# Weights taken apart and put together in alternate steps, block stores ahead of the v and r loads, and unread products between the steps of the first four chains

## Chip, cores and metric

One core of one Trainium2 chip. The metric is the device time of one execution in microseconds (us). "Clock" is TensorE's granted clock as the profile records it, as a share of full speed: 0.50 is half, 1.00 is full.

## The reference, cut to what matters

```python
def _attn_ref(r, k, v, w, a, b):                  # B, H, S, D = 4, 8, 768, 40
    state = zeros((B, H, D, D))
    for t in range(S):
        y[:, :, t] = einsum('bhd,bhde->bhe', rt, state)
        Sa = einsum('bhde,bhe->bhd', state, at)
        state_decay = state * wt[:, :, None, :] - einsum('bhd,bhe->bhde', Sa, bt)
        state = state_decay + einsum('bhd,bhe->bhde', vt, kt)
    return y

def _moe_ref(x, w_in, w_out):                     # x: 3072 x 320, w_in: 320 x 2048, w_out: 2048 x 320
    h = x @ w_in
    return (h / (1 + exp(-h))) @ w_out

out = _moe_ref(y.transpose(0, 2, 1, 3).reshape(B * S, H * D), ...)
```

All of it is in float32.

## The kernel before

The recurrence is cut into 12 chunks of 64 tokens. The parts that matter here are these.

- **Inversion.** For every pair of chunks VectorE (DVE) inverts small triangular blocks row by row (31 rows, two instructions each). Inversion 1 serves chunks 0 and 1, inversion 3 chunks 2 and 3, inversion 5 chunks 4 and 5. Its result goes out to memory and comes back, and TensorE (PE) **merges** it (`pq`, then `po`).
- **Chain.** Each chunk then runs a chain of PE steps: transposes (`pt`), scores (`pm`, `pr`), solve (`pu`, `pw`), update (`pg`), read (`pl`), write (`py`), turn (`pt`). Most of these products are small, 64 rows or 64 columns.
- **MoE.** After every two chunks follow 16 steps with large products: 8 "first" (`ph`) and 8 "second" (`po`).
- **Weights.** 40 pieces arrive as bit patterns of 64-bit floats and are turned into float32 on DVE and ScalarE (ACT).

The order in which steps are written is a proposal: the scheduler that builds the program may place an instruction earlier on its engine if its inputs allow it. That is how MoE products get into PE's waits.

```python
def weave(*lists):                      # mixes lists of steps by their relative position
    at = [(i + 0.5) / len(x) for x in lists for i in range(len(x))]
    steps = [s for x in lists for s in x]
    for i in sorted(range(len(steps)), key=lambda i: at[i]):
        steps[i]()
# ... cut ...
for u in units[0]:
    load_rv(u)                          # loads of r and v
run(prepare(0))
# ... cut ...
run(prepare(1))                         # stores the blocks (md) for inversion 1
# ... cut ...
run(steps[0:1] + convert[0:8] + steps[1:32])            # inversion 1 with 8 weight pieces
# ... cut ...
    weave(late.pop(0) + steps, convert[8:20])           # merge 1 (second half), chain 0
# ... cut ...
    weave(steps[0:4], convert[20:24])                   # chain 1
    weave(steps[4:], convert[24:34], prepare(2))
fetch, queue = moe(0, xs)
# ... cut ...
    weave(queue[0:12], prepare(3) + convert[34:] + invert(3))
del queue[0:12]
for n in range(2, NN):
    # ... cut ...
    steps = [x for pair in zip(*[chain(u, xs) for u in units[n]]) for x in pair]
    steps[4:4] = late.pop(n, [])
    now = 8 if n > 3 else 0
    weave(steps[0:4], queue[0 : now // 4])
    weave(steps[4:], queue[now // 4 : now], prepare(n + 2) + invert(n + 2))
    del queue[0:now]
```

`invert(n)` ends with the merge, so the merge of inversion 5 is written at the end of chain 3.

Of the kernel before, what the change touches and what calls it, by code (L numbers as in the profile page):

```python
# [9 lines left out]
F32 = mybir.dt.float32  # L10
I32 = mybir.dt.int32
U32 = mybir.dt.uint32
# [29 lines left out]
def kernel(  # L42
# [79 lines left out]
    for half in range(2):  # L122
# [6 lines left out]
        for c in range(NF * DM // 2 * half, NF * DM // 2 * (half + 1), WS):  # L129
            pieces.append((wo_f[:, c : c + WS], [(0, 128, w_out[:, 2 * c : 2 * (c + WS)])]))  # L130
    NW = len(pieces)
    rooms = {}

    def load_weights(n):

        if n == 0:
            rooms["gts"] = sb.tile([128, 4, 4 * WS], I32, name="room4", tag="gts")
        if n < NW // 2 and n % 5 < 4:
            rooms[n] = rooms["gts"][:, n % 5]
        else:  # L140
            tag = "room" if n < NW // 2 else ("room", "mi", "tmp")[n % 3]
            rooms[n] = sb.tile([128, 4 * WS], I32, name="room", tag=tag)
        for lo, hi, src in pieces[n][1]:
            raw = rooms[n][lo:hi, 0 : 2 * WS]
            nc.sync.dma_start(raw.rearrange("p (i x) -> p i x", x=256) if len(src.shape) == 3 else raw, src)

    def weights(n):
        dst, room = pieces[n][0], rooms[n]
        words = room[:, 0 : 2 * WS].rearrange("p (c two) -> p c two", two=2)
        lo, hi = words[:, :, 0], words[:, :, 1]  # L150
        e, f = room[:, 2 * WS : 3 * WS], room[:, 3 * WS : 4 * WS]
        shr, band, bor = ALU.logical_shift_right, ALU.bitwise_and, ALU.bitwise_or
        nc.vector.tensor_scalar(out=e, in0=hi, scalar1=20, scalar2=0x7FF, op0=shr, op1=band)
        nc.vector.tensor_scalar(out=f, in0=hi, scalar1=0xFFFFF, scalar2=None, op0=band)
        nc.scalar.activation(out=e, in_=e, func=AF.Relu, scale=2.0**23, bias=low)
        nc.scalar.activation(out=f.bitcast(F32), in_=f, func=AF.Copy, scale=2.0**-20, bias=1.0)  # L156
        nc.scalar.activation(out=lo.bitcast(F32), in_=lo.bitcast(U32), func=AF.Copy, scale=2.0**-52)
        nc.vector.scalar_tensor_tensor(out=e, in0=hi, scalar=-(1 << 31), in1=e, op0=band, op1=bor)
        f, lo, e = (x.bitcast(F32) for x in (f, lo, e))
        nc.vector.tensor_tensor(out=f, in0=f, in1=lo, op=ALU.add)  # L160
        nc.vector.tensor_tensor(out=dst, in0=f, in1=e, op=ALU.mult)
        ahead = 5 if n + 5 < NW // 2 else 3
        if n + ahead < NW and (n + 5 < NW // 2 or n + ahead >= NW // 2):
            load_weights(n + ahead)
# [109 lines left out]

    def inverse(md):
        steps = []
# [21 lines left out]
        def back():  # L298
            nc.sync.dma_start(zd, XI)
            turned = XI.rearrange("p t s -> p s t")  # L300
            nc.scalar.copy(out=mi[:, 0:16], in_=turned[:, 0:16])
            nc.vector.tensor_copy(out=mi[:, 16:32], in_=turned[:, 16:32])
            nc.sync.dma_start(xd, mi)

        steps.append(back)
        return steps, xd, zd

    def merge(n, xd, zd):
        X = XT[n % 2].rearrange("p m h t -> p (m h) t")
# [3 lines left out]
        def fetch():  # L313
            for be in range(2):
                at = 64 * (n % 2) + 32 * be
                nc.sync.dma_start(X[C * be : C * be + 32, :, 32:64], zd[at : at + 16].rearrange("q t s -> t q s"))
                for c in range(2):
                    r = C * be + 32 * c
                    nc.sync.dma_start(
                        X[r : r + 32, :, 32 * c : 32 * c + 32],  # L320
# [319 lines left out]
    def invert(n):  # L640

        if n >= NN or n % 2 == 0:
            return []
        box = {}

        def begin():
            box["rows"], box["xd"], box["zd"] = inverse(md[0])

        def do(k, i):
            if i == 0:  # L650
                box[k] = merge(k, box["xd"], box["zd"])
            box[k][i]()
# [8 lines left out]
    def run(steps):  # L661
        for step in steps:
            step()
# [4 lines left out]
    for n in range(5):  # L668
        load_weights(n)
    convert = [partial(weights, n) for n in range(NW)]  # L670
    xs = dr.tile([DM, 4 * NM * C], F32, name="xs", bufs=2)
    for u in units[0]:
        load_rv(u)
    run(prepare(0))
    for t in RHS + Gbd + GT + XT:
        nc.gpsimd.memset(t, 0.0)
    run(prepare(1))
    chains = {0: [chain(u, xs) for u in units[0]]}
    run([x[i] for i in range(2) for x in chains[0]])
    steps = invert(1)  # L680
    run(steps[0:1] + convert[0:8] + steps[1:32])
    queue = []
    with tc.issue_after(mark["row"]):
# [3 lines left out]
        steps = [x for pair in zip(*[x[2:] for x in chains[0]]) for x in pair]  # L687
        weave(late.pop(0) + steps, convert[8:20])
        for u in units[1]:
# [3 lines left out]
        steps = [x for pair in zip(*[chain(u, xs) for u in units[1]]) for x in pair]  # L693
        weave(steps[0:4], convert[20:24])
        weave(steps[4:], convert[24:34], prepare(2))
    fetch, queue = moe(0, xs)
    fetch()
    with tc.issue_after(mark["turn"]):
        weave(queue[0:12], prepare(3) + convert[34:] + invert(3))
    del queue[0:12]  # L700
    for n in range(2, NN):
# [8 lines left out]
        now = 8 if n > 3 else 0  # L710
        weave(steps[0:4], queue[0 : now // 4])
        weave(steps[4:], queue[now // 4 : now], prepare(n + 2) + invert(n + 2))
        del queue[0:now]
# [160 lines left out]
```

## Time and profile before

| | us |
|---|---|
| median of 3 runs | 977.7 (977.1 to 979.0) |
| the profiled run | 991.1, of the slow state |

The page of the kernel before gives busy time per engine, and then groups of instructions: line, engine, operation, tile written and tiles read, shapes, count, busy us and mean ns, and the engine's idle time just before them.

```profile
PE 849.9 (86%) x10914; PEld 597.4 (60%) x10914; DVE 581.3 (59%) x1045; ACT 281.1 (28%) x628; POOL 92.9 (9%) x90
...
L589 PE MATMUL ph<-xt,wi_s 128*128 128x512 f32 x384 | 197.2, 645 | 30.8 <-DVE gts L598 18.7
L605 PE MATMUL po<-wo_s,gts 128*128 128x320 f32 x768 | 214.5, 436 | 0.0
```

PE is the busiest engine, and over half of its busy time is MoE products (the two groups below and 58.0 us of another first-step group, L594). Note the count of 768: 6 MoE blocks with 8 second steps of 8 products each are 384 products in the source, so **each float32 product leaves two records** in the trace.

### The profile page before, as it was taken

The numbers are of one execution on the slowest core, as the hardware profiler recorded it, in microseconds if no ns is written. First come the engines' busy times: TensorE is split into PE (matmuls) and PEld (weight loads), VectorE is DVE, ScalarE is ACT, GpSimd is POOL, SyncE is SP. The second block draws the span as 40 slices with busy tenths as digits, with TensorE's granted clock in tenths as the row PEclk, the third lists the DMA queues.
The fourth block names the chain that finished last, engine by engine and source line by source line (L and its number), as shares of the span: only waits on it lengthen the run. The fifth ranks groups of instructions, "written<-read, shape, count | busy, mean of one in ns | idle before, by whom it ended". The sixth has DMA issues, their size and how long they took to land. (4 is left out here: it accounts for less than half of the span.)

```text
span 989.2 us, 25109 instructions
## 1 busy us (share of the span) xinstructions
PE 849.9 (86%) x10914; PEld 597.4 (60%) x10914; DVE 581.3 (59%) x1045; ACT 281.1 (28%) x628; POOL 92.9 (9%) x90
## 2 busy tenths in 40 slices
PE   0302989687999778999989999989999999999996
PEld 0302989434489663677745786637867558755544
DVE  8699386998713579526797165991467934031111
ACT  2513453441131412243212433112342033310110
POOL 6101001120000201001120001010020000000000
PEclk9855575899995789999999999999999999999999
DMA  9755255520133560335441345503534133002001
GB/s 227 174 150 138 68 145 133 156 66 17 46 80 95 135 151 13 75 92 126 113 102 56 74 116 125 136 24 76 129 90 115 37 75 82 6 14 58 1 0 30
DMA packets 208948, 87.68 MB, mean 89 GB/s; under 512 B 169408, under 2 KB 199616, under 8 KB 208832
## 3 DMA queue, kind: packets, MB, share of 16 engines
q1 hardware_dynamic: 204608, 84.97, 34.9%
q8 instruction: 87, 1.43, 0.6%
q10 hardware_dynamic: 4224, 1.05, 0.6%
q14 instruction: 29, 0.24, 0.1%
HBM read 68.68 MB, written 17.30 MB: 87 GB/s over the span
## 5 line engine op out<-in xcount | busy, mean ns | idle before, releaser
L589 PE MATMUL ph<-xt,wi_s 128*128 128x512 f32 x384 | 197.2, 645 | 30.8 <-DVE gts L598 18.7
L605 PE MATMUL po<-wo_s,gts 128*128 128x320 f32 x768 | 214.5, 436 | 0.0
L605 PEld LDWEIGHTS po<-wo_s,gts 128*128 128x128 f32 x768 | 143.5, 190 | 64.1 <-issue 3.8
L589 PEld LDWEIGHTS ph<-xt,wi_s 128*128 128x128 f32 x384 | 70.2, 198 | 124.1 <-issue 65.7
L598 DVE TENSOR_TENSOR gts<-ph,sg 128x512 f32<-128x512 f32 x96 | 63.6, 681 | 112.1 <-ACT sg L597 111.9
L597 ACT ACTIVATE sg<-ph 128x512 f32<-128x512 f32 x96 | 52.7, 594 | 226.6 <-PE ph L594 226.6
L286 DVE TENSOR_TENSOR tmp<-XI,mi 128x1 f32<-128x1 f32 (+30 forms) x186 | 100.0, 537 | 11.0 <-DMA mi<-md 6.0
L292 DVE TENSOR_REDUCE XI<-tmp 128x1 f32<-128x1 f32 (+30 forms) x186 | 93.3, 501 | 5.0
L216 PE MATMUL pm<-a,kb 64*64 64x64 f32 x1536 | 45.7, 240 | 39.5 <-POOL kb L248 20.6
L248 POOL TENSOR_TENSOR kb<-kb,w 128x512 f32<-128x512 f32 x42 | 50.4, 1222 | 252.5 <-DVE w L245 185.4
L245 DVE RECIPROCAL w<-W 128x512 f32<-128x512 f32 x21 | 70.3, 3346 | 0.6
L331 PE MATMUL pq<-XT,sb 32*32 32x32 f32 x768 | 26.1, 199 | 50.0 <-DMA XT<-zd 50.0
L216 PEld LDWEIGHTS pm<-a,kb 64*64 64x64 f32 x1536 | 36.8, 148 | 50.8 <-POOL kb L248 41.0
L224 DVE TENSOR_TENSOR sk<-pm,ms 128x256 f32<-128x256 f32 x48 | 18.2, 419 | 82.3 <-PE pm L216 82.3
L246 POOL TENSOR_TENSOR a<-a,W 128x512 f32<-128x512 f32 x24 | 29.1, 1212 | 394.9 <-DMA a<-in_aT 212.4
L515 PE MATMUL pl<-r,vut 64*128 64x64 f32 x768 | 60.6, 310 | 0.0
L507 ACT COPY GT<-pt 40x512 f32<-40x512 f32 x44 | 25.5, 579 | 122.7 <-PE pt L498 121.9
L515 PEld LDWEIGHTS pl<-r,vut 64*128 64x128 f32 x768 | 58.8, 223 | 1.6 <-issue 0.9
L594 PE MATMUL ph<-xt,wl_s 64*128 64x512 f32 x192 | 58.0, 671 | 0.5 <-DMA xt<-xs 0.5
L331 PEld LDWEIGHTS pq<-XT,sb 32*32 32x32 f32 x768 | 23.6, 115 | 56.4 <-ACT room L156 49.9
L485 DVE TENSOR_TENSOR Gbd<-pg,Gbd 64x320 f32<-64x320 f32 x44 | 21.5, 488 | 57.4 <-PE pg L476 56.4
L553 DVE TENSOR_TENSOR yx<-py,W 64x512 f32<-64x512 f32 x48 | 33.0, 688 | 26.2 <-PE py L542 25.4
(97 smaller groups left out, 1026.8 us busy)
## 6 DMA issues: line engine op xcount, KB each, us to landing
a<-in_aT SPq DMA_DIRECT2D x24, 256.0 KB
kb<-in_bT SPq DMA_DIRECT2D x48, 128.0 KB
kb<-in_kT SPq DMA_DIRECT2D x48, 128.0 KB
vut<-in_vT SPq DMA_DIRECT2D x48, 128.0 KB
r<-in_rT SPq DMA_DIRECT2D x24, 256.0 KB
w<-in_wT SPq DMA_DIRECT2D x40, 128.0 KB
room<-in_w_out SPq DMA_DIRECT2D x20, 256.0 KB
room<-in_w_in SPq DMA_DIRECT2D x16, 256.0 KB
```

Source lines behind the costliest of these rows:

```text
L216: nc.tensor.matmul(pm[j][C * be : C * be + C, p * C : p * C + C], lhsT=u.kb[J, q, n, :], rhs=u.a[J, q, :], start=True, stop=True,)
L245: nc.vector.reciprocal(R, u.W[:, :, 1 : C + 1])
L248: nc.gpsimd.tensor_tensor(out=u.kb[:, :, n], in0=u.kb[:, :, n], in1=R, op=ALU.mult)
L286: nc.vector.tensor_tensor(out=tmp[:, 0:n, 0:n], in0=XI[:, t + 1 : 32, t + 1 : 32], in1=mi[:, t, t + 1 : 32].unsqueeze(1).to_broadcast([128 ...
L292: last = nc.vector.tensor_reduce(out=XI[:, t + 1 : 32, t], in_=tmp[:, 0:n, 0:n], axis=AX.X, op=ALU.add)
L331: nc.tensor.matmul(pq[be][r + 32 : r + 64, h * 32 : h * 32 + 32], lhsT=s[r : r + 32, h, 32:64], rhs=X[r : r + 32, h, 32:64], start=True, s ...
L515: nc.tensor.matmul(pl[j][:, q * C : q * C + C], lhsT=u.vut[J, q].rearrange("p n t -> p (n t)"), rhs=u.r[J, q, :], start=True, stop=True,)
L589: in_order(nc.tensor.matmul(ph[n], lhsT=wi_s[:, k, at : at + 128], rhs=xt[:, k, :], start=k == 0, stop=False))
L594: in_order(nc.tensor.matmul(ph[n], lhsT=wl_s[R, i, :], rhs=xt[R, 2, :], start=False, stop=True))
L597: nc.scalar.activation(out=sg, in_=ph[n], func=AF.Sigmoid)
L598: nc.vector.tensor_tensor(out=box["gts"][:, (2 * i + n) % (NF // 2), :], in0=ph[n], in1=sg, op=ALU.mult)
L605: in_order(nc.tensor.matmul(po[:, 0:DM], lhsT=box["gts"][:, f, b * 128 : b * 128 + 128], rhs=wo_s[:, NF // 2 * half + f, :], start=f == 0, ...
```

## The change

The intent is to start the first inversion earlier, to keep VectorE free of conversions while it inverts, and to keep the TensorE clock up in chains 0 to 3 with large products that nobody reads. Five parts:

1. One step takes piece n apart and puts piece n-1 together, so that DVE does not wait for ACT inside a piece; 24 pieces instead of 20 use the early rooms; the first five loads go out on ACT's queue.
2. r and v of the first chunk are loaded after the block stores.
3. Inversion 1's copies use ACT's queue, and merge 1's second half comes four steps into the chain.
4. Conversions are dealt out anew: 6 in inversion 1 (8 before), 13 in chain 0 (12), 7 in chain 1 (14), 15 in the first MoE block (6).
5. **Fillers**: 38 unread products of 512 columns, kept in program order: 10 before merge 1 and one after every second step of chains 0 to 3 (28).

```diff
     def weights(n):
-        # whole piece n: shift, mask, three ACT steps, or, add, multiply
+        if n < NW:
+            # take piece n apart: shift, mask, three ACT steps
+        n -= 1
+        # put piece n-1 together: or, add, multiply
# ... cut ...
-    def inverse(md):
+    def inverse(md, queue):
-            nc.sync.dma_start(xd, mi)
+            queue.dma_start(xd, mi)             # ACT's queue for inversion 1
# ... cut ...
-        load_weights(n)
-    convert = [partial(weights, n) for n in range(NW)]
+        load_weights(n, nc.scalar)
+    convert = [partial(weights, n) for n in range(NW + 1)]
+
+    def busy(x, times=1):
+        for _ in range(times):
+            pj = moe_bank("pj")
+            tc.keep_in_program_order(nc.tensor.matmul(pj, lhsT=ident, rhs=x, start=True, stop=True))
+
+    still = partial(busy, one.rearrange("p q t -> p (q t)")[:, 0:512])
+
+    def with_busy(steps):
+        return [y for i, x in enumerate(steps) for y in ([x, still] if i % 2 else [x])]
# ... cut: load_rv(units[0]) moves behind the start of inversion 1 ...
-    run(steps[0:1] + convert[0:8] + steps[1:32])
+    run(convert[0:6] + steps[1:32])
+    busy(XI.rearrange("p s t -> p (s t)")[:, 0:512], 10)
# ... cut ...
-        weave(late.pop(0) + steps, convert[8:20])
+        steps[4:4] = late.pop(0)
+        weave(with_busy(steps), convert[6:19])
# ... cut ...
-        weave(steps[0:4], convert[20:24])
-        weave(steps[4:], convert[24:34], prepare(2))
+        weave(with_busy(steps[0:4]), convert[19:21])
+        weave(with_busy(steps[4:]), convert[21:26], prepare(2))
# ... cut ...
-        weave(queue[0:12], prepare(3) + convert[34:] + invert(3))
+        weave(queue[0:12], prepare(3) + convert[26:] + invert(3))
# ... cut ...
+        if n < 4:
+            steps = with_busy(steps)
+        cut = 4 if n > 3 else 6
-        weave(steps[0:4], queue[0 : now // 4])
-        weave(steps[4:], queue[now // 4 : now], prepare(n + 2) + invert(n + 2))
+        weave(steps[0:cut], queue[0 : now // 4])
+        weave(steps[cut:], queue[now // 4 : now], prepare(n + 2) + invert(n + 2))
```

More of the change, by code (lines that the diff above doesn't have):

```diff
@@ L130, with load_weights @@
             pieces.append((wo_f[:, c : c + WS], [(0, 128, w_out[:, 2 * c : 2 * (c + WS)])]))
-    NW = len(pieces)
+    NW, NG = len(pieces), 24
     rooms = {}
-    def load_weights(n):
+    def load_weights(n, queue=nc.sync):
         if n == 0:
             rooms["gts"] = sb.tile([128, 4, 4 * WS], I32, name="room4", tag="gts")
-        if n < NW // 2 and n % 5 < 4:
+        if n < NG and n % 5 < 4:
             rooms[n] = rooms["gts"][:, n % 5]
         else:
-            tag = "room" if n < NW // 2 else ("room", "mi", "tmp")[n % 3]
+            tag = "room" if n < NG else ("room", "mi", "tmp")[n % 3]
             rooms[n] = sb.tile([128, 4 * WS], I32, name="room", tag=tag)
@@ L144, in load_weights, with parts @@
             raw = rooms[n][lo:hi, 0 : 2 * WS]
-            nc.sync.dma_start(raw.rearrange("p (i x) -> p i x", x=256) if len(src.shape) == 3 else raw, src)
-    def weights(n):
-        dst, room = pieces[n][0], rooms[n]
-        words = room[:, 0 : 2 * WS].rearrange("p (c two) -> p c two", two=2)
-        lo, hi = words[:, :, 0], words[:, :, 1]
-        e, f = room[:, 2 * WS : 3 * WS], room[:, 3 * WS : 4 * WS]
-        shr, band, bor = ALU.logical_shift_right, ALU.bitwise_and, ALU.bitwise_or
-        nc.vector.tensor_scalar(out=e, in0=hi, scalar1=20, scalar2=0x7FF, op0=shr, op1=band)
-        nc.vector.tensor_scalar(out=f, in0=hi, scalar1=0xFFFFF, scalar2=None, op0=band)
-        nc.scalar.activation(out=e, in_=e, func=AF.Relu, scale=2.0**23, bias=low)
-        nc.scalar.activation(out=f.bitcast(F32), in_=f, func=AF.Copy, scale=2.0**-20, bias=1.0)
-        nc.scalar.activation(out=lo.bitcast(F32), in_=lo.bitcast(U32), func=AF.Copy, scale=2.0**-52)
+            queue.dma_start(raw.rearrange("p (i x) -> p i x", x=256) if len(src.shape) == 3 else raw, src)
+    shr, band, bor = ALU.logical_shift_right, ALU.bitwise_and, ALU.bitwise_or
+    def parts(n):
+        words = rooms[n][:, 0 : 2 * WS].rearrange("p (c two) -> p c two", two=2)
+        return words[:, :, 0], words[:, :, 1], rooms[n][:, 2 * WS : 3 * WS], rooms[n][:, 3 * WS : 4 * WS]
+    def weights(n):
+        if n < NW:
+            lo, hi, e, f = parts(n)
+            nc.vector.tensor_scalar(out=e, in0=hi, scalar1=20, scalar2=0x7FF, op0=shr, op1=band)
+            nc.vector.tensor_scalar(out=f, in0=hi, scalar1=0xFFFFF, scalar2=None, op0=band)
+            nc.scalar.activation(out=e, in_=e, func=AF.Relu, scale=2.0**23, bias=low)
+            nc.scalar.activation(out=f.bitcast(F32), in_=f, func=AF.Copy, scale=2.0**-20, bias=1.0)
+            nc.scalar.activation(out=lo.bitcast(F32), in_=lo.bitcast(U32), func=AF.Copy, scale=2.0**-52)
+        n -= 1
+        if n < 0:
+            return
+        lo, hi, e, f = parts(n)
         nc.vector.scalar_tensor_tensor(out=e, in0=hi, scalar=-(1 << 31), in1=e, op0=band, op1=bor)
@@ L160, in weights @@
         nc.vector.tensor_tensor(out=f, in0=f, in1=lo, op=ALU.add)
-        nc.vector.tensor_tensor(out=dst, in0=f, in1=e, op=ALU.mult)
-        ahead = 5 if n + 5 < NW // 2 else 3
-        if n + ahead < NW and (n + 5 < NW // 2 or n + ahead >= NW // 2):
+        nc.vector.tensor_tensor(out=pieces[n][0], in0=f, in1=e, op=ALU.mult)
+        ahead = 5 if n + 5 < NG else 3
+        if n + ahead < NW and (n + 5 < NG or n + ahead >= NG):
             load_weights(n + ahead)
@@ L302, in back, with merge @@
             nc.vector.tensor_copy(out=mi[:, 16:32], in_=turned[:, 16:32])
-            nc.sync.dma_start(xd, mi)
+            queue.dma_start(xd, mi)
         steps.append(back)
         return steps, xd, zd
-    def merge(n, xd, zd):
+    def merge(n, xd, zd, queue):
         X = XT[n % 2].rearrange("p m h t -> p (m h) t")
@@ L318, in fetch @@
                     r = C * be + 32 * c
-                    nc.sync.dma_start(
+                    queue.dma_start(
                         X[r : r + 32, :, 32 * c : 32 * c + 32],
@@ L644, in invert @@
         box = {}
+        queue = nc.scalar if n == 1 else nc.sync
         def begin():
-            box["rows"], box["xd"], box["zd"] = inverse(md[0])
+            box["rows"], box["xd"], box["zd"] = inverse(md[0], queue)
         def do(k, i):
             if i == 0:
-                box[k] = merge(k, box["xd"], box["zd"])
+                box[k] = merge(k, box["xd"], box["zd"], queue)
             box[k][i]()
@@ L668 @@
     for n in range(5):
-        load_weights(n)
-    convert = [partial(weights, n) for n in range(NW)]
+        load_weights(n, nc.scalar)
[7 more added lines that the diff above has]
+        return [y for i, x in enumerate(steps) for y in ([x, still] if i % 2 else [x])]
     xs = dr.tile([DM, 4 * NM * C], F32, name="xs", bufs=2)
-    for u in units[0]:
-        load_rv(u)
     run(prepare(0))
@@ L677 @@
     run(prepare(1))
+    steps = invert(1)
+    run(steps[0:1])
+    for u in units[0]:
+        load_rv(u)
     chains = {0: [chain(u, xs) for u in units[0]]}
     run([x[i] for i in range(2) for x in chains[0]])
-    steps = invert(1)
-    run(steps[0:1] + convert[0:8] + steps[1:32])
+    run(convert[0:6] + steps[1:32])
+    busy(XI.rearrange("p s t -> p (s t)")[:, 0:512], 10)
     queue = []
```

## The prediction

> **What bounds the kernel now.** I read the forty-slice strip first, because it shows where the engines change roles; then a table of busy time by stage, cut where one kind of work ends on VectorE (DVE) or TensorE (PE); then PE's waits; then the timelines around the worst places. The strip, one digit per 24.7 us, in tenths:
>
> ```profile
> PE   0302989687999778999989999989999999999996
> ...
> DVE  8699386998713579526797165991467934031111
> ...
> PEclk9855575899995789999999999999999999999999
> ```
>
> PE is nearly empty for four slices while DVE is full. PE is then full at a granted clock of about a half, dips near slices 7 to 9, and from about slice 17 on is full at full clock. The stage table has for each stretch its length, the busy us (and instruction count) of PE, weight load, DVE, ACT and POOL, then clock, DMA share and GB/s:
>
> ```profile
> 45.80:83.00 37.20, 0.00 (x0) 0.00 (x0) 35.27 (x78) 5.45 (x14) 0.00 (x0) 0.50 0.49 127
> 83.00:105.60 22.60, 13.20 (x258) 12.96 (x258) 16.07 (x37) 11.77 (x25) 3.87 (x3) 0.50 0.56 152
> 105.60:180.00 74.40, 70.94 (x1072) 68.16 (x1072) 50.90 (x120) 34.24 (x87) 4.01 (x3) 0.61 0.48 128
> 180.00:283.90 103.90, 86.49 (x423) 44.88 (x418) 81.38 (x144) 31.03 (x69) 12.11 (x10) 0.92 0.27 66
> 283.90:360.30 76.40, 68.66 (x1507) 64.13 (x1504) 33.88 (x55) 22.08 (x51) 9.36 (x8) 0.75 0.44 106
> 360.30:424.00 63.70, 53.91 (x261) 27.67 (x261) 46.82 (x75) 14.18 (x29) 4.89 (x4) 0.92 0.31 73
> 424.00:989.20 565.20, 544.81 (x7136) 369.20 (x7134) 282.59 (x478) 146.25 (x314) 38.27 (x32) 0.99 0.30 73
> ```
>
> In order: the first triangular inversion (DVE alone), merging its result, chains 0 and 1, the first MoE block with inversion 3, chains 2 and 3, inversion 5, and the rest. PE bounds the chains, at a reduced clock; DVE bounds the inversions; after 424 us PE is busy 544.8 of 565.2 us, so **any PE work pushed behind that point adds its full length**. The wait view and two timelines carry the rest:
>
> ```profile
> PE pq L331 <- DMA XT<-zd: 50.0, 2, 49.8
> ```
> ```profile
> 92.90 3.35 DVE L245 RECIPROCAL w<-W 128x512 f32<-128x512 f32 x1
> 97.03 0.58 ACT L341 COPY qq<-pq 32x512 f32<-32x512 f32 x1
> 153.55 12.20 PE L515 MATMUL pl<-r,vut 64*128 64x64 f32 x64
> 442.78 3.79 PE L515 MATMUL pl<-r,vut 64*128 64x64 f32 x64
> ```
>
> PE waits 49.8 us for the first merge. Inside it ACT, in order, sits behind a 3.35 us reciprocal before it can evacuate the second merge product. The same 64 products take 12.20 us at half clock and 3.79 us at full clock. The profiled run took 991 us, the unprofiled median is 977.7; I work in the trace's time and carry differences over.
>
> **What the Trainium skill says.** "TensorE: Matmul & The Clock Gate", Part 1, has an idle PE at 1.2 GHz and a busy one at 2.4 GHz after about 3.4 us. The trace agrees on two levels (0.50 and 1.00) but not on what counts as busy: from 100 to 120 us PE is 100% busy with 64-row products at 0.50. [...]The same page, Part 2 (step 1), keeps matmuls in program order, only weight loads being pulled ahead; the 49.8 us wait agrees. "DMA: Bandwidth & Descriptors", "Issuing engines are not separate DMA queues", says that a second issuing engine saves only issue time: here that is 3.55 us for six weight loads and about 9 us for the r and v loads that stand before the 16 block stores (`md`). "Advanced Engine Details and Errata", "VectorE Performance Modes", says GpSimd and two-port VectorE instructions block each other: the conversion's first step has median 0.285 us and maximum 1.27 us.
>
> **The change, part by part.**
> (1) *Blocks ahead of r and v.* The last score is ready at 31.2 us; four stores at 0.57 us each and the weights' `w` reach 34.1; the read-back's second half goes after the last store has landed, about 36.1, and lands 3.8 us later as now. Inversion 1 starts at about 40 instead of 45.8: **-6**.
> (2) *Fewer conversions inside inversion 1.* Its 62 row instructions are 31.4 us busy plus about 2 us of gaps; with 1.3 us of other work it ends at about 75 instead of 83 (2 us gained).
> (3) *Merge.* The copies back go out on ACT's queue, and only the first merge precedes the first solve. Result read-back 6.5 us, ten filler products during it, one merge at full clock and the copies: 13.5 us instead of 22.6, so the solve starts near 88 instead of 105.6: **-17**.
> (4) *Chains 0 and 1.* At full clock a chain pair costs PE 28.4 us including its merge (after 424: 544.8 minus 34 first products at 4.82 and 36 second products at 4.36, over 8 pairs). From 88: 56 us of PE work with 13 fillers at 0.47, against 76 us of DVE work counted from 75 on. With some 10 us of stalls: end at about 156 instead of 180: **-24**.
> (5) *First MoE block.* 15 conversions, about 2 us each, fall here instead of 6 to 9. Summing the row durations in the order of the built program, DVE has 47.7 us before inversion 3 and 39.1 us inside it, plus 4 us of waits: inversion 3 ends at 247 instead of 267.4. Chain 2 starts 12 us later, 259 instead of 283.9: **-25**.
> (6) *Chains 2 and 3.* Now 76.4 us, of which about 33 us are at half clock (16 us to be won) and 7.7 us idle. With 15 fillers at 0.47 (+7) and 2 us more waiting: about 70; end 329 instead of 360.3: **-31**.
> (7) *What the fillers lock out.* They are kept in program order, so nothing written after them in the source can be placed before them. Comparing the two built programs' PE order: before, by chain 4's first transpose 14 first and 12 second steps of the MoE are done; after, 8 and 4.75. None stands between chain 3 and the merge that needs inversion 5. DVE then needs 42 us for inversion 5 and read-back and merge 14 more: chain 4 starts at 329 + 42 + 14 = 385 instead of 424: **-39**, with PE idle for some 45 us which the kernel before fills with MoE products.
> (8) *The bill.* 6 first steps at 4.82 (28.9) and 7.25 second steps at 4.36 (31.6): **+60** behind chain 4, where PE is full. Of 20 us idle there some 6 may be filled by them: -6.
> Sum: -39 + 60 - 6 = +15. Parts (4) and (6) may each be 4 to 8 us better than I assume, hence +8 as my middle.
>
> **Rivals.** *A: the early gain reaches the end.* For it: 58.6 us of PE time are lost to the half clock (busy time times missing clock, summed over 10 us stretches), and PE idles 88 us before 106. Against it: part (7); to be 2% faster chain 4 would have to start near 350, while DVE's row durations up to the end of inversion 5 already sum to 312 us and chain 4 needs 14 more, with no idle DVE at all. It would make about 940 to 955. *B: the fillers do not hold the clock.* One of 0.45 us in every 4 to 5 us. Against it: from 424 on the clock is 0.99 although single MoE pairs are 10 us apart. If it held, parts (4) and (6) shrink by 20 us and the time is about 1005. *C: DVE bounds more than I sum*, by waits for weight loads with only three rooms in the first MoE block, or by GpSimd conflicts: 5 to 10 us later, about 995. *D: the locked-out MoE work fits into later waits of PE.* The order after chain 4 spreads it into the chains, but only 13 us of PE idleness before the tail is there to be filled; it is in the sum.
>
> **Range and chances.** Middle 986, from +8. The sum of seven stages, each good to 3 to 8 us, gives about 15 us either way; B and C stretch the upper side, A's milder forms the lower: 964 to 1006. Faster by over 2% (under 958) needs an error in (7) or (8): 0.12. Slower by over 2% (over 997): 0.28. Same: 0.60.
>
> **What would show it.** Inversion 1 from 40 to 75; first solve near 88; clock close to 1.00 from there to chain 4, but for the gaps in which PE idles; end of chain 1 near 156; chain 2's transposes near 259; chain 3's end near 329; then a PE wait of about 45 us for the inversion, absent before; chain 4 near 385; and from there 620 us to the end instead of 565. If PE works on the MoE between chains 3 and 4, or if the rest takes under 600 us, (7) or (8) is wrong and the kernel is faster than I say. If the clock stays at a half in chains 0 to 3, B is right.

## More of the kernel before

A run counts as slow when it is over 1.5% above the fastest run of the same kernel.

## The result and the profile after

The changed kernel is correct and takes **1031.6 us** (median of 4 runs, 1030.9 to 1036.8) against 977.4 us in the same rounds. The ratio is 1.0574, with a 95% interval from 1.0524 to 1.0624: slower by 5.7%, and outside the predicted range. Ratios here are the mean time of one kernel's fast runs over that of the other's fast runs of the same rounds, in the experiments without the profiled runs, so they are not quite the ratio of the quoted medians.

The strip of the changed kernel, one digit per 25.7 us, in tenths:

```profile
PE   0418996892996506999998999999999999999997
...
DVE  8997686988053792163597164893446934122211
...
PEclk9757688996698856999999999899999999999999
```

PE has a hole in slices 14 and 15 (digits 5 and 0) that the kernel before has not, and the clock falls to 5 and 6 tenths in slices 15 and 16. (The 2 in slice 10 is a shorter wait, 20.7 us, for inversion 3.) From then on PE is full to the end. In slices 4 to 13 the clock is better than before in places, but not 1.00.

The views of PE's waits and of PE's instructions in order of time show the hole. The timeline columns are start, us, engine, line, tiles, shapes, count, and in brackets the idle time before and its releaser.

```profile
PE pq L339 <- DMA XT<-zd: 68.1, 2, 47.4
```
```profile
106.41 7.09 PE L523 MATMUL pl<-r,vut 64*128 64x64 f32 x64
...
394.74 3.40 PE L339 MATMUL pq<-XT,sb 32*32 32x32 f32 x64 [47.36 <-DMA XT<-zd]
398.07 2.08 PE L685 MATMUL pj<-one,ident 128*128 128x512 f32 x2
399.94 2.31 PE L613 MATMUL po<-wo_s,gts 128*128 128x320 f32 x5
```

PE stands idle for 47.4 us until inversion 5 is back, does that merge's first products, then **one filler**, and only then an MoE product (`po`). And at 106 us the 64 `pl` products take 7.09 us, at a clock of 0.50. So they do in chain 2 of the kernel before, in its first profile and also at 0.50:

```profile
305.84 7.09 PE L515 MATMUL pl<-r,vut 64*128 64x64 f32 x64
```

That is close to twice the 3.79 us at full clock. The 12.20 us which the prediction called half clock (chain 1, also recorded at 0.50) are more than half a clock explains; what made them so long is not known.

Because the first profile of the kernel before was of a slow run, I profiled it again (the first experiment). Its busy times by stage, with the columns of the prediction's stage table; the rows are the start up to the first solve, chains 0 and 1, from there to chain 2 (first MoE block, inversion 3), chains 2 and 3, from there to chain 4 (inversion 5), and chain 4 to the end:

```profile
0.00:105.12 105.12, 24.34 (x529) 22.78 (x529) 85.89 (x175) 33.21 (x79) 24.30 (x33) 0.70 0.68 162
105.12:172.95 67.83, 64.07 (x1074) 61.26 (x1072) 51.39 (x120) 34.37 (x88) 3.97 (x3) 0.71 0.52 141
172.95:276.05 103.10, 85.62 (x418) 45.08 (x417) 81.60 (x144) 30.98 (x69) 12.07 (x10) 0.90 0.26 66
276.05:348.53 72.48, 64.62 (x1507) 60.41 (x1504) 33.75 (x55) 22.03 (x51) 9.36 (x8) 0.81 0.46 112
348.53:412.25 63.72, 53.77 (x261) 27.65 (x261) 46.86 (x75) 14.22 (x29) 4.88 (x4) 0.92 0.32 73
412.25:977.20 564.95, 544.51 (x7137) 369.25 (x7134) 282.53 (x478) 146.30 (x314) 38.24 (x32) 0.99 0.30 73
```

The same six stages of the changed kernel:

```profile
0.00:89.25 89.25, 28.74 (x421) 20.65 (x421) 82.53 (x164) 26.19 (x64) 24.10 (x33) 0.76 0.78 179
89.25:163.86 74.61, 70.96 (x1225) 56.50 (x1225) 54.77 (x122) 38.72 (x98) 7.43 (x6) 0.76 0.50 133
163.86:265.15 101.29, 68.52 (x355) 34.68 (x355) 77.00 (x150) 33.18 (x75) 8.29 (x7) 0.83 0.29 74
265.15:347.39 82.24, 72.98 (x1534) 58.92 (x1532) 35.23 (x60) 22.24 (x51) 9.35 (x8) 0.88 0.42 101
347.39:406.50 59.11, 11.76 (x142) 8.75 (x142) 40.79 (x60) 7.14 (x15) 4.88 (x4) 0.57 0.27 65
406.50:1029.20 622.70, 602.83 (x7321) 402.46 (x7318) 287.71 (x492) 153.82 (x328) 39.07 (x32) 0.99 0.27 68
```

The first solve comes 16 us earlier. Chains 0 and 1, and chains 2 and 3, each take longer than before although their clock is higher. PE does 11.8 us of work in the 59.1 us ahead of chain 4, against 53.8 of 63.7. And what was not done there comes after chain 4: 622.7 us instead of 565.0, with PE busy for 602.8 instead of 544.5. These are 58 us more of PE work at the end; chain 4 starts 5.7 us earlier than before, so 52 us of loss are left between these two traces.

### The profile page after: what moved, and what is told of

It reads as the page before. It is cut to its first block, busy times and chain, and to the rows that moved or that the text cites. A ratio compares the mean times of both kernels' runs of the same rounds, so it can differ in the third digit from the quotient of the medians.

```text
span 1029.2 us, 25272 instructions
## 1 busy us (share of the span) xinstructions
PE 855.8 (83%) x10990; PEld 582.0 (57%) x10990; DVE 578.0 (56%) x1045; ACT 281.3 (27%) x628; POOL 93.1 (9%) x90
## 4 chain that ended last, share of the span: by engine, by line
PE 62%; DVE 28%; DMA 4%; issue 2%; ACT 2%; SPq 0%; POOL 0%; ACTq 0%; DVEq 0%; POOLq 0%
PE po L613 16%; PE ph L597 12%; DVE tmp L294 8%; DVE XI L300 7%; DVE w L253 4%; PE ph L602 4%; PE pj L685 3%; PE pl L523 3%; PE pu L446 3%; PE pm L224 2%; PE py L550 2%; PE pr L424 2%; PE py L543 2%; PE pq L339 2%; PE pg L484 2%
## 5 line engine op out<-in xcount | busy, mean ns | idle before, releaser
L613 PE MATMUL po<-wo_s,gts 128*128 128x320 f32 x768 | 218.5, 439 | 1.2 <-DVE gts L606 1.2
L597 PE MATMUL ph<-xt,wi_s 128*128 128x512 f32 x384 | 186.7, 624 | 9.6 <-DVE gts L606 9.5
L597 PEld LDWEIGHTS ph<-xt,wi_s 128*128 128x128 f32 x384 | 70.0, 194 | 96.5 <-issue 69.3
L339 PE MATMUL pq<-XT,sb 32*32 32x32 f32 x768 | 23.6, 200 | 68.1 <-DMA XT<-zd 68.1
L339 PEld LDWEIGHTS pq<-XT,sb 32*32 32x32 f32 x768 | 21.4, 115 | 76.3 <-issue 54.3
L523 PEld LDWEIGHTS pl<-r,vut 64*128 64x128 f32 x768 | 48.0, 200 | 6.2 <-issue 5.8
L523 PE MATMUL pl<-r,vut 64*128 64x64 f32 x768 | 49.1, 285 | 0.0
L625 DVE TENSOR_TENSOR ot<-po,ot 128x320 f32<-128x320 f32 x24 | 11.7, 487 | 66.5 <-PE po L613 66.5
## 6 DMA issues: line engine op xcount, KB each, us to landing
a<-in_aT SPq DMA_DIRECT2D x24, 256.0 KB
r<-in_rT SPq DMA_DIRECT2D x24, 256.0 KB
room<-in_w_out SPq DMA_DIRECT2D x20, 256.0 KB
```

The source lines that it names most:

```text
L339: nc.tensor.matmul(pq[be][r + 32 : r + 64, h * 32 : h * 32 + 32], lhsT=s[r : r + 32, h, 32:64], rhs=X[r : r + 32, h, 32:64], start=True, s ...
L523: nc.tensor.matmul(pl[j][:, q * C : q * C + C], lhsT=u.vut[J, q].rearrange("p n t -> p (n t)"), rhs=u.r[J, q, :], start=True, stop=True,)
L597: in_order(nc.tensor.matmul(ph[n], lhsT=wi_s[:, k, at : at + 128], rhs=xt[:, k, :], start=k == 0, stop=False))
L613: in_order(nc.tensor.matmul(po[:, 0:DM], lhsT=box["gts"][:, f, b * 128 : b * 128 + 128], rhs=wo_s[:, NF // 2 * half + f, :], start=f == 0, ...
```

## The experiments

**The theory** at this point: the fillers are fences, MoE work cannot be placed ahead of them, so it is missing in the wait for inversion 5 and paid behind chain 4. **Rivals**: the fillers' own time on PE (37.2 us for the 28, in their group of the trace); the conversions that were moved, or the weights in alternate steps. Each kernel below was correct and was timed in three rounds on one chip with the kernel before, unless told otherwise; its runs were fast but for two of kernel 2 and one of kernel 8. Slow runs of the kernel before are left out. All of them in one table, by stage as above (us in the trace of one run; "ratio" is to the kernel before). A stage stands on one trace: four traces of kernels without fillers and with the old deal of conversions (before twice, 11 and 14) have 67.3 to 76.4 us for chains 2 and 3, so differences of that size there prove nothing alone.

| kernel | first solve at | chains 0, 1 | to chain 2 | chains 2, 3 | to chain 4 | chain 4 to end | median | ratio (95%) |
|---|---|---|---|---|---|---|---|---|
| before, again | 105.1 | 67.8 | 103.1 | 72.5 | 63.7 | 565.0 | 979.0 | one run |
| changed | 89.3 | 74.6 | 101.3 | 82.2 | 59.1 | 622.7 | 1031.6 | 1.057 (1.052 to 1.062) |
| 1 no fillers | 88.1 | 62.9 | 105.1 | 80.4 | 63.1 | 573.1 | 972.4 | 0.998 (0.989 to 1.006) |
| 2 fillers of 4 columns | 89.0 | 64.6 | 105.8 | 72.8 | 62.1 | 622.7 | 1023.9 (mean of 2 fast runs) | 1.053 (worked out) |
| 3 none in chains 2, 3 | 89.0 | 74.7 | 102.6 | 76.5 | 64.3 | 568.2 | 979.8 | 1.009 (1.003 to 1.015) |
| 4 all free of the order | 92.7 | 53.8 | 110.5 | 66.6 | 64.0 | 564.5 | 956.2 | 0.983 (0.977 to 0.990) |
| 5 before + fillers | 106.0 | 73.8 | 88.4 | 83.0 | 55.7 | 623.3 | 1031.9 | 1.057 (1.051 to 1.064) |
| 6 free, chains 2, 3 only | 88.5 | 62.6 | 111.8 | 65.7 | 65.5 | 561.0 | 956.8 | 0.982 (0.975 to 0.988) |
| 7 free, early ones only | 94.2 | 55.1 | 105.8 | 78.7 | 64.3 | 565.1 | 966.0 | 0.994 (0.986 to 1.002) |
| 8 free, 9 late | 92.8 | 52.7 | 107.3 | 73.5 | 62.8 | 568.0 | 959.4 (3 fast runs) | 0.980 (0.970 to 0.990) |
| 9 the 28 doubled | 89.6 | 81.3 | 85.4 | 89.0 | 57.8 | 626.2 | 1026.3 | 1.049 (1.040 to 1.057) |
| 10 before + free fillers | 114.1 | 64.2 | 104.5 | 69.3 | 63.7 | 562.3 | 980.4 | 1.003 (0.996 to 1.011) |
| 11 before + blocks ahead | 99.5 | 68.0 | 103.0 | 76.3 | 63.7 | 565.5 | 972.5 | 0.993 (0.985 to 1.001) |
| 12 last filler out | 88.8 | 76.1 | 101.1 | 148.7 for both | | 578.8 | 993.7 | 1.019 (1.013 to 1.025) |
| 13 one filler, 4 columns | 88.5 | 58.4 | 105.2 | 74.3 | 63.0 | 622.6 | 1012.5 | 1.040 (1.032 to 1.047) |
| 14 before + alternate weights | 104.5 | 68.6 | 103.4 | 67.3 | 64.1 | 562.9 | 973.9 | 0.999 (0.991 to 1.006) |

### A second profile of the kernel before

No edit, one run.

> The kernel before, unchanged, for a profile in the fast state, because its first profile was of a slow run (991 us against a median of 977). Expected 971 to 978 us; if the stages scale, chain 4 begins near 415 instead of 424 and takes 558 to 566 us from there to the end.

It took 979.0 us, 1 us over the expected band, and its state is unknown because it is one run. Set beside the stage table in the prediction, the first solve (105.6 there), the time to chain 2 (103.9), the time to chain 4 (63.7) and the rest (565.2) are the same within 1 us. Most of the 12 us between the two spans lies in chains 0 and 1 (74.4 there, at a clock of 0.61) and chains 2 and 3 (76.4, at 0.75). So in these two runs of one kernel it is mostly the clock in the chains that differs, and chain 4 starts at 412, not at 424 as the prediction took it.

### 1. No fillers

```diff
-    busy(XI.rearrange("p s t -> p (s t)")[:, 0:512], 10)
-        return [y for i, x in enumerate(steps) for y in ([x, still] if i % 2 else [x])]
+        return [y for i, x in enumerate(steps) for y in [x]]
```

> The changed kernel without any of its 38 unread products (ten before the first merge, 28 between chain steps); all else as changed. Theory (fence): the loss is what the products lock out, so without them chain 4 should find 13 to 14 first and 12 second MoE steps done, the 47 us wait for inversion 5 is filled again, and the time falls to 962 to 978 us (977 before; about 12 us come from the earlier inversion 1 and the shorter merge). Rival (moved conversions): the 15 conversions in the first MoE block keep DVE late, and the time stays above 1000 us. Rival (weights in alternate steps cost more): above 990 us.

972.4 us. The loss is gone, and the moved conversions and the alternate weights are not its cause. Chain 4 starts at 399.5, 13 us before the kernel before, and yet the ratio is 0.998: chains 2 and 3 take 80.4 us, and the rest is 8 us longer in this trace than in the others with the same PE work (a dip of the clock between 760 and 790 us, which I can't explain).

### 2. Fillers of 4 columns

```diff
-            tc.keep_in_program_order(nc.tensor.matmul(pj, lhsT=ident, rhs=x, start=True, stop=True))
+            tc.keep_in_program_order(nc.tensor.matmul(pj[:, 0:4], lhsT=ident, rhs=x[:, 0:4], start=True, stop=True))
```

> The changed kernel with every unread product cut from 512 columns to 4: the same places in the program order (8 first and 5 second MoE steps before chain 4), next to no PE time[...]. Theory (fence): the order alone costs 40 to 55 us over the kernel without fillers, so 1005 to 1030 us, with PE idle for 45 us or more ahead of inversion 5's merge. Rival (the products' own time on PE is the cause): within 10 us of the kernel without fillers, 965 to 985 us, and no such wait.

Its four runs took 1018.9, 1028.9, 1036.9 and 1038.0 us; the last two count as slow beside the first. The mean of the fast ones is 1023.9 us, inside the expected band and 1.053 times the 972.5 us of the fast runs of before. That is 8 us below the changed kernel. The ratio on record is 1.063 (1.054 to 1.072): it leaves out the profiled run, 1018.9, and then counts the other three as fast. PE's wait view and the last stage of this kernel:

```profile
PE pq L339 <- DMA XT<-zd: 99.0, 3, 48.5
```
```profile
394.38:1017.10 622.72, 601.87 (x7315) 401.13 (x7312) 287.25 (x491) 153.80 (x328) 39.12 (x32) 0.99 0.27 68
```

Same wait, same 622.7 us from chain 4 to the end. The **order alone** makes most of the loss. The fillers' own length has about 8 us in it by the first count and none by the second. The profiled run was the fastest of the four.

### 3. Fillers only up to chain 1

```diff
-        if n < 4:
-            steps = with_busy(steps)
```

> The changed kernel with unread products only before the first merge and in chains 0 and 1 (23 of 38); none in chains 2 and 3, so MoE work can be placed there again (13.5 first and 12 second steps before chain 4). Theory (fence): close to the kernel without fillers, 955 to 978 us, PE's wait for inversion 5 under 15 us. Rival (own time of the products): only 15 of 38 are gone, so about 1010 us.

979.8 us, 2 us over the band. Without fillers in chains 2 and 3 the rest falls to 568.2. The 23 early ones cost something: this ratio is 1.1% above that of run 1, from the same rounds, and chains 0 and 1 take 74.7 us instead of 62.9.

### 4. All fillers, but free of the program order

```diff
-            tc.keep_in_program_order(nc.tensor.matmul(pj, lhsT=ident, rhs=x, start=True, stop=True))
+            nc.tensor.matmul(pj, lhsT=ident, rhs=x, start=True, stop=True)
```

> The changed kernel with the same 38 unread products of 512 columns, but not kept in program order: they can be placed anywhere and no longer hold anything back (14 first and 12 second MoE steps before chain 4). Theory (fence): 968 to 998 us, since up to 28 products of 1.06 us at full clock may still lie on PE's path, but no wait for inversion 5 over 15 us. Rival (own time): as slow as the changed kernel, 1015 to 1035 us.

956.2 us: better than the theory's own band, and faster than both kernels, by 1.7% (clear of noise, but below the 2% of a verdict). The scheduler gathered the fillers: the ten and then seven more around merge 1, and 15 ahead of the second steps of the first MoE block; the other six lie in and just before chains 0 and 1. The fillers use the same PSUM banks as the MoE products (`moe_bank`), here as in the changed kernel; so holding these banks, a rival not named so far, doesn't make the loss. The chains 0 and 1 of this kernel, and the `pl` products and the gathered fillers in its timeline:

```profile
92.67:146.43 53.76, 51.00 (x1211) 44.31 (x1210) 44.87 (x107) 36.72 (x92) 3.50 (x3) 0.97 0.58 156
```
```profile
104.47 3.79 PE L523 MATMUL pl<-r,vut 64*128 64x64 f32 x64
...
224.93 12.28 PE L685 MATMUL pj<-one,ident 128*128 128x512 f32 x28 [1.30 <-DVE gts L606]
```

Chains 0 and 1 run at a clock of 0.97 and take 53.8 us, and `pl` takes 3.79 us at 104 us, against 7.09 in the changed kernel. In a row a filler takes 12.28 us over 14 products (28 records), that is **0.88 us**.

### 5. The kernel before plus the fillers alone

The edit is the definition of `busy`, `still` and `with_busy` as in the diff of the change, and their use at the same places; nothing else of the change.

> The kernel before with nothing of the change but the 38 unread products kept in program order (37 of them ahead of chain 4). Theory (fence): they alone make the loss, whatever the other parts: 1020 to 1045 us, 8 first and 5 second MoE steps before chain 4, PE idle over 40 us for inversion 5, some 620 us from chain 4 to the end. Rival (the loss needs the later conversions as well): under 1000 us.

1031.9 us and a ratio of 1.0574, that of the changed kernel to the last digit. The fillers make the whole loss on the old schedule too.

### 6 and 7. Only the late, or only the early fillers, free of the order

```diff
 # 6: no ten before merge 1, chains 0 and 1 without with_busy; not kept in order
 # 7: the ten and chains 0 and 1 only; not kept in order
```

> The changed kernel with unread products in chains 2 and 3 only, not kept in order; the built order gathers all 15 in the first MoE block, between the last first step and the second steps, so that second steps fill the wait for inversion 3. Theory (PE enters chain 2 without an idle stretch and so at full clock, which saves the 13 us by which chain 4 came earlier): 952 to 962 us, clock 1.00 over chain 2. Rival (the 23 early products make the gain): 968 to 976 us, like the kernel without any.

> The changed kernel with the ten and the 13 unread products of chains 0 and 1 only, not kept in order; the built order gathers 17 of them around the first merge. Theory (chains 0 and 1 run at full clock, but inversion 3 on DVE sets when chain 2 starts, so the gain is waited away): 966 to 977 us, chain 2 near 256 us. Rival (the early gain reaches the end): 952 to 962 us.

956.8 and 966.0 us, both as the theory had it. The late ones make most of the gain. The stretch in which chain 2 begins suggests how, first in the kernel without fillers (run 1), then in run 4:

```profile
244.00:249.00 5.00, 0.16 (x4) 0.19 (x5) 0.42 (x2) 1.06 (x1) 0.00 (x0) 0.79 0.69 240
249.00:260.00 11.00, 10.56 (x157) 10.06 (x158) 0.00 (x0) 4.34 (x8) 0.00 (x0) 0.50 0.43 67
256.01:293.78 37.77, 36.30 (x819) 34.25 (x817) 12.55 (x23) 10.89 (x23) 2.36 (x2) 0.76 0.39 98
```
```profile
244.00:249.00 5.00, 5.00 (x47) 3.60 (x46) 0.49 (x1) 0.58 (x1) 0.00 (x0) 1.00 0.79 123
249.00:260.00 11.00, 11.00 (x178) 8.79 (x176) 0.95 (x3) 3.78 (x7) 0.00 (x0) 1.00 0.11 18
256.90:288.16 31.26, 30.78 (x828) 27.59 (x825) 13.10 (x25) 10.50 (x23) 2.36 (x2) 1.00 0.49 124
```

Without fillers PE has done its MoE work too early and idles for 5 us before inversion 3 comes back. The clock falls to 0.50, and chain 2, made of small products, takes 37.8 us at 0.76. With the late fillers gathered ahead of the second steps, these are still there to fill the wait, and chain 2 takes 31.3 us at 1.00; chain 3, too, is shorter (35.3 us instead of 42.6). That the clock on entering chain 2 is the cause is not shown: no run changed it alone. Nor does a full clock on entering always last. The kernel before enters chain 2 at 1.00 in both of its traces; in the first it then ran at 0.50 from 294 to 316 us with PE busy all the time, in the second at 0.92 in the 22 us from the same point on (286 to 308 us). The early fillers (run 7) shorten chains 0 and 1 to 55.1 us, but the first solve is 6 us later and chain 2 starts at 255.0, where it started without them (256.0): inversion 3 sets that.

### 8. Nine late fillers instead of 15, free of the order

```diff
-        return [y for i, x in enumerate(steps) for y in ([x, still] if i % 2 else [x])]
+        # in chains 2 and 3 after every third step only
```

> The changed kernel with all unread products free of the program order as before, and those of chains 2 and 3 cut from 15 to 9 (one after every third step). Theory (what counts is that PE enters chain 2 without an idle stretch; products beyond that only cost 1.06 us each): 6 fewer products, chain 2 still entered at full clock and up to 6 us earlier, 948 to 957 us, faster than the kernel before by about 2.5%. Rival (all 15 are needed): 960 to 972 us, with clock 0.5 early in chain 2.

959.4 us is the median of the fast runs (955.5 to 960.9; one slow run took 980.3), between the two expectations and so **inconclusive**. Chain 2 started 4 us earlier and took 30.4 us, as fast as with 15. But chains 2 and 3 together took 73.5 us at a clock of 0.81, so chain 3 (43.1 us, against 35.3 in run 4) lost what chain 2 had won.

### 9. Each of the 28 fillers twice, in order

```diff
-    still = partial(busy, one.rearrange("p q t -> p (q t)")[:, 0:512])
+    still = partial(busy, one.rearrange("p q t -> p (q t)")[:, 0:512], 2)
```

> The changed kernel, in program order, with each of the 28 unread products between chain steps issued twice (1024 columns in all). Theory (spread through a chain they cost more PE time than the clock gives back; 512 instead of 4 columns cost 12 us up to chain 4): 1040 to 1062 us, some 620 us from chain 4 to the end as before. Rival (there were only too few to hold the clock): clock 0.95 or more in chains 0 and 1, chain 4 before 400 us, under 1025 us.

1026.3 us. **My theory missed here**: twice the filler work did not cost 10 us or more, it cost nothing. The rival missed too: the clock in chains 0 and 1 was 0.86, chain 4 came at 403, and the time is above 1025, if barely. Chains 0 to 3 became longer by 13.4 us together in spite of a better clock (0.86 and 0.95), as I had thought, but the time to chain 2 became 16 us shorter: the order of the conversions on DVE shifted, with 66.9 us of DVE work inside chains 0 and 1 instead of 54.8 and less behind them. With 4, 512 and 1024 columns the kernel takes 1023.9, 1031.6 and 1026.3 us, in different rounds (ratios 1.053 or 1.063, 1.057 and 1.049). The length of the fillers is not what decides the time; their place is.

### 10. The kernel before plus free fillers

The edit of run 5 with that of run 4.

> The kernel before with only the 38 unread products, free of the program order. Theory (the gain comes from the filled waits, not from the other parts of the change): 955 to 968 us, and chain 2 entered at full clock. Rival (it needs the earlier inversion and the conversions moved): 970 us or more.

980.4 us. **This misses my theory**: the gain of run 4 does not come from filled waits alone. Chains 2 and 3 do run at a clock of 1.00 here (69.3 us), but chain 2 starts at 282.7, against 256.9 in run 4. In run 10 the scheduler put fillers among the merge products of chunk 0 and of chunk 1, ahead of the first solve, and the first solve came 9 us later than in the kernel before. The earlier chain 2 comes from the other parts of the change: without any filler, run 1 starts it at 256.0, the kernel before at 276.1. Which of them does it was not tested.

### 11. The kernel before plus blocks ahead of r and v

```diff
-    for u in units[0]:
-        load_rv(u)
     run(prepare(0))
# ... cut ...
+    steps = invert(1)
+    run(steps[0:1])
+    for u in units[0]:
+        load_rv(u)
```

> The kernel before with only the stores of the blocks sent ahead of the loads of v and r (the read-back too). Prediction's step 1: inversion 1 starts at about 40 instead of 45.8 us and the first solve comes 6 us earlier, near 99 us. To the end: within 1% of before (967 to 978), because inversion 3 on DVE and the full PE behind chain 4 decide; rival (the early gain reaches the end in full): 971 us and chain 4 6 us earlier.

The first solve came at 99.5 us, 5.6 us earlier, as the prediction's step 1 had it. 972.5 us and 0.993 (0.985 to 1.001) cannot tell a gain of 6 us from none. In its trace chain 4 starts at 410.6, 1.7 us earlier than in the second profile of before.

### 12 and 13. Which filler is the fence

By now it was known that the order makes the loss. In the order of the built program one filler stands out, the last of chain 3. `weave` sorts steps by relative position: that filler is the last of 15 steps (14.5 / 15 = 0.967), and the merge's first products are the 40th of 41 (39.5 / 41 = 0.963). So it lands just behind products that wait for inversion 5, and everything written later must wait with it.

```diff
 # 12: the changed kernel, 37 of its 38 fillers
             steps = with_busy(steps)
+            if n == 3:
+                del steps[-1]
 # 13: run 1 (no fillers), plus a single one of 4 columns at that place
+        ahead = prepare(n + 2) + invert(n + 2)
+        if n == 3:
+            ahead[-1:-1] = [still]
```

> The changed kernel with one of its 38 unread products taken out, the last of chain 3; the other 37 stay, in program order. In the built order 12.2 first and 12 second MoE steps are then done before chain 4, against 8 and 4.8. Theory (one product in front of which PE waits for inversion 5 locks the work out): 4.2 times 4.82 plus 7.2 times 4.36, some 51 us, come back: 975 to 990 us, PE's wait for inversion 5 under 10 us, some 572 us from chain 4 to the end. Rival (the 28 as a whole): within 5 us of the changed kernel.

> The changed kernel without its unread products, but with a single one of 4 columns kept in program order right behind the first products of the merge that needs inversion 5 (8 first and 5.1 second MoE steps are then done before chain 4, as in the changed kernel). Theory: that one instruction of under 0.2 us costs as much as all 38: 1010 to 1032 us, PE idle 45 us or more for inversion 5, some 622 us from chain 4 to the end. Rival (number or length of the products): 966 to 980 us, as without any.

Run 12: 993.7 us, somewhat above its band. One filler less brings 38 us back. The rest is 578.8 us, and PE's wait for inversion 5 is gone from its view; a wait of 20.8 us for inversion 3 stays:

```profile
PE pq L339 <- DMA XT<-zd: 20.8, 1, 20.8
```
```profile
414.67:993.50 578.83, 556.52 (x7155) 374.92 (x7152) 283.24 (x480) 147.87 (x316) 38.05 (x32) 0.99 0.29 72
```

Run 13: 1012.5 us, inside its band. Its PE timeline and its last stage:

```profile
375.19 3.40 PE L339 MATMUL pq<-XT,sb 32*32 32x32 f32 x64 [48.81 <-DMA XT<-zd]
378.53 0.59 PE L685 MATMUL pj<-one,ident 128*128 128x4 f32 x2
```
```profile
389.38:1012.00 622.62, 602.72 (x7315) 401.83 (x7312) 287.59 (x491) 153.82 (x328) 39.09 (x32) 0.99 0.27 68
```

**A single product of 0.6 us, in the wrong place, costs 40 us** (1012.5 against 972.4), with a wait of 48.8 us and 622.6 us at the end, where 38 fillers have 47.4 and 622.7. The remaining part of the loss, some 20 us (993.7 against 972.4), is that of the other 37. Longer chains and second steps kept from the wait for inversion 3 are likely parts of it; how it divides I have not measured.

### 14. The kernel before plus alternate weights

The edit is part 1 of the change, but for the queue of the first loads, and nothing else of it.

> The kernel before with only the weights taken apart and put together in alternate steps (and 24 pieces with five rooms). Theory: fewer waits of DVE for ACT inside the conversion, but DVE is not the bound behind chain 4 and inversions decide before it: 968 to 980 us, within 1% of before. Rival (DVE saves a microsecond or more for each of 40 pieces ahead of chain 4): under 960 us.

973.9 us, 0.999: no effect that three rounds could show.

## Why the prediction was wrong

- **Steps 1 to 3 were right.** Inversion 1 ran from 38.7 to 73 us (predicted 40 to 75) and the first solve came at 89.3 (88). (One count of rival A is off, without consequence: before the first solve PE idles 80.5 us, 105.58 less 25.05 busy, not 88.)
- **Steps 7 and 8, the lock-out and its bill, were right in kind and size.** The wait for inversion 5 was 47.4 us (predicted about 45) and the rest 622.7 us (620). What the prediction didn't see is that one filler does most of it; "nothing written after them in the source can be placed before them" is true of all 28, but 27 of them leave MoE work free to go into the long wait (run 12).
- **Step 4 failed: "At full clock a chain pair costs PE 28.4 us ... 13 fillers at 0.47".** Predicted 68 us for chains 0 and 1, measured 74.6 at a clock of 0.76. Two terms were wrong. First, a filler was priced by one of its two records: thirteen of them were busy 18.5 us in that stretch, 1.42 us each instead of 0.47, or 12 us more. Second, a filler every few us did not hold the clock. The price of a chain pair was about right (redone, its sum gives 28.0 us, not 28.4): with gathered fillers the clock was 0.97, PE was busy for 51.0 us and the stage took 53.8 (run 4).
- **The ground for step 4 was a wrong reading.** A sentence cut from the prediction had it that large products lift the clock, by the example of 128x128 transposes at 131 us. In that trace the clock is at 1.00 from 129 us on, behind products of 64 columns, and the transposes begin at 131.2. In the second trace of the same kernel it rises from 0.50 to 1.00 near 110 us, with only products of up to 64 columns since 97 us. What raises the clock stays open; gathered fillers went with 0.97, spread ones with 0.76, spread ones of double length with 0.86 (run 9). The 12.20 us of `pl` read as half clock were the other wrong reading: at 0.50 these products take 7.09 us.
- **Step 6 failed in the same way**: 70 us predicted, 82.2 measured, at 0.88; 14 of its 15 fillers were busy 16.7 us in it, where 7 were planned for all. Steps 4 and 6 together are 19 of the 21.5 us by which chain 4 came later than predicted (406.5 against 385); inversion 5 adds 3.1 us, the first solve 1.3, and step 5 was 1.7 us short. This is rival B, "the fillers do not hold the clock", whose 20 us were named and then not believed.
- **The sum failed by its base line.** The stages added up to 385 + 620 = 1005 us of trace. I set that against the slow run's 989 instead of an ordinary run's 977, and so carried +15 to a median to which it didn't belong: 13 us of the miss. Then I rounded +15 to +8 because two parts "may each be 4 to 8 us better than I assume": nearly another 8 (385 + 620 is 15.8 us over the 989.2). With 24 us from the stages (1029.2 against 1005) this is the 45.6 us between 986 and 1031.6. Without these two choices the same working gives about 1006.
- **Was a filler's own time the cause?** Not for the sign: with 4 columns in place of 512 at least 46 of the 54 us stay (1023.9 against 977.4, run 2). It was a mis-sized term of the stages, while the lock-out decided the sign.
- **Rival A**, the early gain reaching the end, came true in a milder form in run 4, where nothing locks MoE work out and PE isn't idle on entering chain 2: chain 4 starts at 387.5 us, and the time is 956.2 us (ratio 0.983). With runs 6 and 8 it is one of the versions that beat both kernels.
- **Rivals C and D** stayed small: inversion 5 came 3.1 us late and step 5 was 1.7 us short (C, 5 to 10 us); the rest took 622.7 us, so no locked-out work vanished in later waits (D).

## What to carry to other kernels

An instruction pinned to its place on an in-order engine is a fence for all work written after it: before adding one, look in the built order at which wait stands right before it, and what would otherwise have filled that wait. Look for an engine that goes idle just before a stretch of small work: here unread load gathered ahead of that stretch went with a shorter one (runs 4 and 6), load sprinkled through it did not shorten it. And check the state of the run a profile was taken from before carrying stage times over to a median.

## What the Trainium skill lacked or had wrong

- "TensorE: Matmul & The Clock Gate", Part 1, has the clock full after about 3.4 us of sustained work. In the kernel before PE was busy for 20.00 of 20.00 us (100 to 120 us) at 0.50, in the changed kernel for 14.18 of 15.00 us (105 to 120 us) at 0.50. The same `pl` products also ran at 1.00 (3.79 us, run 4). In the kernel before, chain 2 fell from 1.00 to 0.50 behind an idle gap of 0.69 us and stayed there for 22.00 us with PE busy for all 22.00 (294 to 316 us); in its second trace, behind a gap of 0.74 us, it had 0.92 over the 22 us that followed (286 to 308 us). The page does not say how products this small count.
- The same page, "HAM oscillation", warns of idle gaps above about 3.4 us. The runs agree: 5 us of idleness took the clock to 0.50. What it lacks is how long this lasts with small products behind it: 0.50 over 11 us in which PE was busy for 10.56 (run 1, 249 to 260 us), and 0.76 over the whole of chain 2.
- "FP8 and Floating Point Precision", "TensorE Precision Notes", has four passes for true FP32. The trace shows two records per product, and the prediction took one of them for the whole. Four passes of 512 columns at the 2.4 GHz of the clock page would be 0.85 us, an estimate from these two pages; the runs show 0.88 us in a row. The pages lack the remark that a trace splits such a product in two.
- No page says what an isolated float32 product of 512 columns costs among small ones (the latency of a single product on the clock page is for bf16): 1.42 us on average in chains 0 and 1 of the changed kernel, at a clock of 0.76.
